# A long convolution with experts: 54 columns combined in the main loop, a ninth place for x, and another order of blocks

## The chip, the cores and the metric

The kernel runs on one core of a Trainium2 chip. Times are microseconds of device time, lower is better. The engines are named as in the profile: PE is TensorE's matmul (PEld its weight loads), DVE is VectorE, ACT is ScalarE, POOL is GpSimd, and SP is the queue from which nearly all transfers are issued.

## The reference

Inputs are `x` and `v` of 4 batches, 12608 positions and 128 channels, all float32. A small network over positions makes one long filter for each channel; `x * v` is convolved with it and gated with `x`, and then 128 positions of each batch, those with the highest scores, go through a two-layer expert.

```python
h = (np.maximum(pos_emb @ w1, 0) @ w2) * np.exp(-0.01 * pos)[:, None]
u = x * v
L = 2 * S
y = np.fft.irfft(np.fft.rfft(u, n=L, axis=1) * np.fft.rfft(h, n=L, axis=0)[None], n=L, axis=1)[:, :S]
a = x * y
scores = np.einsum('bsd,d->bs', a, w_gate)
for b in range(4):
    top = np.argpartition(-scores[b], 128)[:128]
    g = 1 / (1 + np.exp(-scores[b, top]))
    a[b, top] += g[:, None] * (np.maximum(a[b, top] @ mw1, 0) @ mw2)
```

## The kernel before

**Stages.** The Fourier transforms are written as matrix products over a grid of 101 x 250 points. After the filter's own transform (to about 120 us) comes the *main loop*: 128 steps, 32 for each of the 4 batches, each step with 4 channels. A step on PE is `f_s1` (L426), `dft` (L268) and, three steps later for the same channels, `f_i` (L263). DVE multiplies by the filter (L432 to L447). GpSimd has five instructions a step: `f_sd` (L453, L454), the product `x * v` for a later step (`stage_u`, L249), and `f_c` (L496, L497).

`f_i` leaves its result in PSUM; ACT copies it to `big`, which is read as `ay` (L477), and the last columns' second half to a small buffer `stg` (L478). For each of 126 columns `ay` holds two parts, called C and S here. `f_c` replaces them, for the columns from `JM` on, by their difference and sum. `JM` is 80 before, so these are 46 columns, 184 elements for 4 channels.

**The column loop** (class `P1`, once for each batch, after the batch's 32nd `f_i`) makes the second transform, column by column. The columns lie in 16 blocks of 8 (the last has 6), a block in two half-blocks of 4; `h` counts half-blocks in the order in which they are done, and the table `ORD` is the order of the blocks. A column whose sum and difference are there needs two products (L542); any other needs four (L546). In the profile every float32 product is two records, so 4 or 8 passes a column. For the blocks below `JB` the four middle columns are combined inside the loop, by `comb` on GpSimd (L529, two instructions of 512 elements a block), into one of two rooms of `cm`, in turn. `CB` lists these blocks in order.

For each half-block `fin` multiplies with x on DVE (L557). When a block is complete it is written out (L580, a transfer of 420 KB on SP). Then the scores are made: `weigh` multiplies with the gate's weights (L591), on DVE, or on GpSimd for the half-blocks that are `far`: those of the blocks from 10 on, but for the ones in `DW`. ACT sums each column (`sums`, L601, two records a column). For `h` of 28 and more the sums are put off into the next main loop, except in the last batch.

**Rooms for x.** The blocks of x are loaded (L519) into rooms listed in `XB`, by place in the order: one room in `wx`, five in `xa`, and two (`XE`) that lie in buffers of the main loop. Blocks whose first room isn't one of `XE` are loaded ahead, in halves, one half in each of the steps of the main loop that `LA` names; the two in `XE` when the loop begins; the others when an earlier block's write has left the room.

**What sets the order.** Everything is written in program order, and each engine's queue and SP's run in that order; the waits between them follow from the memory that the instructions touch. Besides GpSimd's waits for the loop's data, a load or a combination into a room waits for the write that still reads it. PE has four places in PSUM for half-blocks in the column loop (three in the last batch). While the main loop of one batch runs, the top-128 search of the batch before it is strung into its steps on PE, DVE and ACT, and gathers its rows by a transfer on GpSimd's queue (L899).

The second pass of rooms `XB[i]`, and the first writes of buffers that are read before they are full, need cleared memory; ACT clears these rooms in the first three steps (L1059, L1063).

Of the kernel before, what the change touches and what calls it, by code (L numbers as in the profile page):

```python
# [17 lines left out]
B, S, D, FO = 4, 12608, 128, 64  # L18
# [11 lines left out]
HB = 4  # L30
# [7 lines left out]
NU, NV, NX, NH = 4, 2, 5, 3  # L38
# [2 lines left out]
PJ = (N3 + 1) // 2  # L41
NC, CO = 4, 2
NE = 3
LA = range(32 - 14, 32 - 2)
NS, ND = 64, 4
NWARM = 8
JB = 10
JM = 8 * JB
ORD = (0, 10, 1, 2, 11, 3, 4, 12, 5, 6, 13, 7, 8, 14, 9, 15)
CB = [k for k in ORD[1:] if k < JB]  # L50
PC = 4
NL, NM = 28, 7
DW = (2, 14)
OFF, _o = {}, 0
for _n, _k, _w in (("te", 2, 2 * HC), ("qs", 2, HC), ("mt", 1, 2 * HC), ("yz", 2, 2 * HC), ("ws", 1, 728), ("sd", 2, 2 * HC),
                   ("ht", NH, 2 * HC), ("xa", NX, 8 * D), ("wx", 2, HB * D), ("cm", 2, 2 * NC * D), ("x", NU, XC), ("v", NV, XC)):
# [4 lines left out]
XE = [CE, OFF["yz"][0] + 2 * HC]  # L61
CE = [XE[0] + 8 * D, XE[1] + 8 * D]
XB = [OFF["xa"][0] + k * 8 * D for k in range(NX)] + XE
XB = [OFF["wx"][0]] + [XB[(i + NX - 2) % (NX + 2)] for i in range(len(ORD) - 1)]
AHEAD = [i for i in range(NX + 3) if XB[i] not in XE]
POS0, HID0 = 0, PJ * N1


# [95 lines left out]
def hyena_moe(ctx, tc, xg, x2, pos, bw, ww, wg, mw1, mw2, fo, c1, gx, cf, ci, wm, tk, out):  # L164
# [66 lines left out]
    blk = [c for c, _, _ in _steps()[1]]  # L231
# [267 lines left out]
    blocks = [(j0, min(j0 + 8, NJ)) for j0 in range(0, NJ, 8)]  # L499
    hbs = [(ja, min(HB, z - ja)) for a, z in (blocks[k] for k in ORD) for ja in range(a, z, HB)]  # L500

    class P1:
# [46 lines left out]
        def fin(self, h):  # L549
            ja, n = self.hbs[h]  # L550
            blk = ja // 8
            xa = self.xa[blk]
            js = slice(ja % 8, ja % 8 + n)
            end = self.last and n == 2
            if end:
                self.weigh()
            nc.vector.tensor_tensor(out=xa[:, js], in0=self.s4.pop(h)[:, :n], in1=xa[:, js], op=ALU.mult)  # L557
            if not end:
                self.weigh()
                far = ja >= JM and n == HB and h not in DW  # L560
                if h >= NL and not self.last:
                    o = OFF["cm"][0] + 2 * NC * D if h < 30 else OFF["wx"][0]
                    wx = view(arena, o + h % 2 * HB * D, [128, HB, D])
                elif far:
                    wx = view(arena, CE[self.pw % 2], [128, HB, D])
                    self.pw += 1
                else:
                    wx = view(arena, self.wx[2 + self.nw % 2 if self.nw < 6 else (self.nw - 6) % 4], [128, HB, D])
                    self.nw += 1
                self.mul = xa[:, js], wx[:, :n], ja, n, far, h  # L570
                if far:
                    self.weigh()
            else:
                for k in range(n):
                    nc.vector.scalar_tensor_tensor(out=junk, in0=xa[:, ja % 8 + k], scalar=1.0,
                                                   in1=self.wg, op0=ALU.mult, op1=ALU.mult,
                                                   accum_out=self.sc[:, ja + k:ja + k + 1])
            if ja + n == blocks[blk][1]:
                j0, j1 = blocks[blk]
                nc.sync.dma_start(out[self.b, :, j0:j1], xa[P0:P0 + PR, :j1 - j0])  # L580
                i = ORD.index(blk)
                if i > 1:
                    self.load_a(i - 1 + NX + len(XE))
                if blk in CB:
                    self.comb()

        def weigh(self):
# [19 lines left out]
        def run(self, ex):  # L607
            self.last = ex is not None
            self.ring = (0, 1, 2) if ex else (3, 2, 0, 1)
            self.wx = [OFF["wx"][0], OFF["wx"][0] + HB * D, OFF["te"][0] + (2 * HC if ex else 0),  # L610
                       OFF["sd"][0] if ex else OFF["ht"][0] + ((self.b + 1) * NG + 2) % NH * 2 * HC]
            self.wg = ps2(1, [128, D], f"wg_{self.b}")
            nc.scalar.copy(out=self.wg, in_=wgb)
            for i in range(NX + 3):
                if i not in AHEAD:
                    self.load_a(i)
            for k in range(2):
                self.comb()
            for h in range(len(self.hbs)):
                self.mm(h)  # L620
                self.fin(h)
                if h == 29:
                    stage_u((self.b + 1) * NG + 5)
                if ex:
                    ex.hook(h, self.wg)
            self.weigh()
            if ex:
                self.mask()
# [411 lines left out]
    for t in range(NT + LAG):  # L1040
        g = t % NG
        i = t - LAG
        if 0 <= i:
            f_i(i, sd.pop(i))
        if t < NT:
            pq = ps2(1 - t % 2, [128, 2, 512], f"pq_{t}")
            spare[0] = [a[:, 512 - NS:] for a in bank1]
            uv[t] = pq[:, :, :HC]
            bg.now = t
            qs = dft(t, te.pop(t), (uv[t][:, 0], uv[t][:, 1]))  # L1050
            bg.hook("p", 1)
            bg.hook("n", 1)
            if t + 1 < NT:
                te[t + 1] = f_s1(t + 1)
            spare[0] = None
            bg.hook("w", 1)
            load_u(t + NU)
            for k in range(2 * t, min(2 * t + 2, NX)):
                nc.scalar.activation(out=buf("xa", k, [128, 8 * D]), in_=one.to_broadcast([128, 8 * D]), func=AF.Copy,  # L1059
                                     scale=0.0)  # L1060
            if t == 2:
                for o, w in ((XB[0], 8 * D), (OFF["ws"][0], 728)):
                    nc.scalar.activation(out=view(arena, o, [128, w]), in_=one.to_broadcast([128, w]), func=AF.Copy,  # L1063
                                         scale=0.0)
            o = t - 1 in uv
            if o:
                y = f_y(t - 1, uv[t - 1], f_m(t - 1, uv.pop(t - 1)))
            f_v(uv[t], qs)
            for _ in range(ND):
                bg.hook("d")  # L1070
            f_u(uv[t], qs)
            seam = i >= 0 and i % NG == NG - 1
            if seam:
                f_c(i)
            if o or t - 1 in ys:
                sd[t - 1] = f_sd(t - 1, y if o else ys.pop(t - 1))
            if i < 0 or i % NG < NG - 1:
                stage_u(t + 3)
            if i >= 0 and not seam:
                f_c(i)  # L1080
            if t:
                load_h(t + 2)
            for _ in range(NE):
                bg.hook("e")
            if i >= 0 and i % NG == NG - 1:
                ys[t] = f_y(t, uv[t], f_m(t, uv.pop(t)))
            if t == NT - 1:
                sd[t] = f_last(t, uv.pop(t))
# [13 lines left out]
        b = i // NG  # L1102
        if i >= 0 and i % NG in LA:
            if i % NG == LA[0]:
                ph[b] = P1(b)
            k, e = divmod(LA.index(i % NG), 2)
            ph[b].load_a(AHEAD[k], e * HB, (e + 1) * HB)
# [59 lines left out]
```

## Time and profile before

| | |
|---|---|
| time, median of 3 runs | 899.78 us (898.28 to 901.48) |
| the profiled execution | 897.32 us, span 895.5 us |
| PE, PEld | 865.7 us (97%), 763.4 us (85%) |
| DVE, POOL, ACT | 807.6 us (90%), 763.9 us (85%), 627.9 us (70%) |
| chain that ended last | PE 71%, DVE 16%, ACT 5%, POOL 4% |
| DMA | 195.06 MB, mean 218 GB/s |

The times are of whole executions; the span is what the profile covers, the rest lies before and after it. Busy shares are averages over stages that differ: the transform of the filter, the main loop with its four column loops, and the end of the last batch.

### The profile page before, as it was taken

The page shows a single profiled execution, that of the slowest core. Times are in us where ns is not written, and L with a number is a line of the kernel's source. Part 1 is how long each engine was busy: PE and PEld are TensorE (multiplying, and loading weights), DVE is VectorE, ACT ScalarE, POOL GpSimd, SP SyncE. Part 2 cuts the span into 40 slices and gives each one's busy share as a digit, 9 for nine tenths or more (in the row PEclk, how much of TensorE's full clock was granted, in tenths as well). Part 3 has the DMA queues.
Part 4 walks back from the last instruction along what each step waited for, and adds up shares of the span by engine and source line. Part 5 has one row for each costly group of instructions (what it writes and reads, how often), then busy time and mean ns, then how long its engine had stood idle before and what let it go on. Part 6 is the DMA issues. An engine that isn't in the chain of part 4 may idle for free.

```text
span 895.5 us, 46412 instructions
## 1 busy us (share of the span) xinstructions
PE 865.7 (97%) x19606; PEld 763.4 (85%) x19606; DVE 807.6 (90%) x1543; ACT 627.9 (70%) x2242; POOL 763.9 (85%) x834
## 2 busy tenths in 40 slices
PE   8999989999999999999999999999999999999965
PEld 6788768999999889888899798888998898879954
DVE  8998899999999899999998898999998989997883
ACT  6655575555558988885579798855698888646920
POOL 5898659999999889898999798999998989988710
PEclk9999999999999999999999999999999999999996
DMA  7044587777887967688779766788797767855810
GB/s 251 35 174 172 205 291 226 213 217 230 262 248 246 296 219 220 200 247 250 243 234 299 224 213 207 231 247 236 250 300 237 221 199 227 253 176 179 267 60 7
DMA packets 83512, 195.06 MB, mean 218 GB/s; under 512 B 9639, under 2 KB 46608, under 8 KB 83304
## 3 DMA queue, kind: packets, MB, share of 16 engines
q1 hardware_dynamic: 83048, 191.57, 67.6%
q8 instruction: 154, 2.52, 1.1%
q0 software_dynamic: 256, 0.52, 0.2%
q14 instruction: 54, 0.44, 0.2%
HBM read 151.46 MB, written 40.60 MB: 214 GB/s over the span
## 4 chain that ended last, share of the span: by engine, by line
PE 71%; DVE 16%; ACT 5%; POOL 4%; issue 3%; DMA 2%; POOLq 0%; DVEq 0%; SPq 0%; ACTq 0%
PE c L263 19%; PE a L426 15%; PE c L268 15%; ACT arena L601 4%; PE c L546 3%; PE a L542 3%; PE a L546 3%; PE c L542 3%; PE c L402 2%; PE a L382 2%; DVE arena L440 2%; DVE c L441 2%; PE c L382 2%; DVE arena L446 1%; DVE ms L696 1%
## 5 line engine op out<-in xcount | busy, mean ns | idle before, releaser
L263 PE MATMUL c<-ci_sb,arena 128*26 128x126 f32 x8128 | 261.0, 271 | 2.1 <-POOL arena L453 1.6
L263 PEld LDWEIGHTS c<-ci_sb,arena 128*26 128x26 f32 x8128 | 244.7, 104 | 5.1 <-POOL arena L453 1.8
L268 PE MATMUL c<-arena,cf_sb 128*32 128x404 f32 x2048 | 214.0, 502 | 3.3 <-ACT arena L428 1.3
L426 PE MATMUL a<-c_sb,arena 128*32 128x202 f32 (+1 forms) x4096 | 216.1, 334 | 0.0
L426 PEld LDWEIGHTS a<-c_sb,arena 128*32 128x32 f32 (+1 forms) x4096 | 174.5, 108 | 26.7 <-issue 12.8
L249 POOL TENSOR_TENSOR arena<-arena 128x500 f32<-128x500 f32 x128 | 161.9, 1265 | 11.3 <-DMA arena<-in_xg_dram 11.3
L428 ACT COPY arena<-a 128x404 f32<-128x404 f32 x256 | 128.1, 501 | 50.2 <-PE a L426 48.8
L477 ACT COPY big<-c 128x824 f32<-128x824 f32 x127 | 106.3, 837 | 78.2 <-PE c L263 77.9
L453 POOL TENSOR_TENSOR arena<-arena 128x404 f32<-128x404 f32 x127 | 124.0, 977 | 39.0 <-DVE arena L447 30.7
L601 ACT ACTIVATE arena<-arena 128x128 f32<-128x128 f32 x502 | 147.4, 299 | 11.7 <-DVE arena L591 9.5
L268 PEld LDWEIGHTS c<-arena,cf_sb 128*32 128x32 f32 x2048 | 100.8, 109 | 35.6 <-issue 18.8
L440 DVE TENSOR_TENSOR arena<-c,arena 128x808 f32<-128x808 f32 x127 | 126.8, 998 | 3.8
L441 DVE TENSOR_TENSOR c<-c,arena 128x808 f32<-128x808 f32 x127 | 126.7, 998 | 0.0
L454 POOL TENSOR_TENSOR arena<-arena 128x404 f32<-128x404 f32 x127 | 123.6, 973 | 0.0
L601 ACT ACTIVATION_READ_ACCUMULATOR arena<-arena 128x1 f32 x502 | 96.0, 191 | 0.0
L529 POOL TENSOR_TENSOR arena<-big 128x512 f32<-128x512 f32 x72 | 89.8, 1285 | 0.7 <-PE c L542 0.4
L446 DVE TENSOR_TENSOR arena<-c,arena 128x404 f32<-128x404 f32 x127 | 73.6, 579 | 12.9
L435 DVE TENSOR_TENSOR c<-c,arena 128x404 f32<-128x404 f32 x128 | 74.6, 583 | 11.6 <-ACT arena L271 8.2
L432 DVE TENSOR_TENSOR c<-c,arena 128x404 f32<-128x404 f32 x128 | 75.0, 586 | 9.6 <-ACT c L765 4.9
L497 POOL TENSOR_TENSOR big<-big,arena 128x184 f32<-128x184 f32 x128 | 74.5, 582 | 10.0
L271 ACT COPY arena<-c 128x404 f32<-128x404 f32 x128 | 63.6, 497 | 24.2 <-PE c L268 23.1
L496 POOL TENSOR_TENSOR big<-big,arena 128x184 f32<-128x184 f32 x128 | 75.0, 586 | 1.3 <-ACT arena L478 1.3
(196 smaller groups left out, 1433.5 us busy)
## 6 DMA issues: line engine op xcount, KB each, us to landing
arena<-in_xg_dram SPq DMA_DIRECT2D x256, 250.0 KB, 3.9
arena<-hd SPq DMA_DIRECT2D x128, 404.0 KB, 4.5
out_dram<-arena SPq DMA_DIRECT2D x60, 420.0 KB, 5.4
arena<-in_x_dram SPq DMA_DIRECT2D x36, 420.0 KB, 4.7
hd<-arena SPq DMA_DIRECT2D x32, 404.0 KB, 3.0
arena<-in_x_dram SPq DMA_DIRECT2D x48, 210.0 KB, 5.0
arena<-in_pos_dram SPq DMA_DIRECT2D x15, 202.0 KB, 4.5
arena<-in_x_dram SPq DMA_DIRECT2D x4, 315.0 KB, 4.5
```

The source lines that it names most:

```text
L249: nc.gpsimd.tensor_tensor(out=x, in0=x, in1=v, op=ALU.mult)
L263: nc.tensor.matmul(o[32 * k:32 * k + c.stop - c.start], lhsT=lhsT[:, c], rhs=rhs, start=True, stop=True)
L268: nc.tensor.matmul(pq[w][a:a + 32], lhsT=cf_sb[:, 2 * w + a // NQ, a % NQ:a % NQ + 32], rhs=te[:, a // NQ], start=True, stop=True)
L426: nc.tensor.matmul(tps[s // 2][c, s % 2], lhsT=u[:, s, c], rhs=c1_sb[:, 0:k + 2:k + 1], start=True, stop=True)
L428: nc.scalar.copy(out=te[:, :, 2 * h:2 * h + 2].rearrange("p e s i -> p s e i"), in_=tps[h])
L440: nc.vector.tensor_tensor(out=mt, in0=uv, in1=ht[:, 0].unsqueeze(1).to_broadcast([128, 2, HC]), op=ALU.mult)
L441: nc.vector.tensor_tensor(out=uv, in0=uv, in1=ht[:, 1].unsqueeze(1).to_broadcast([128, 2, HC]), op=ALU.mult)
L453: eng.tensor_tensor(out=nat(sd[:, 0]), in0=nat(yz[:, 0]), in1=rev(yz[:, 1]), op=ALU.add)
L454: eng.tensor_tensor(out=nat(sd[:, 1]), in0=rev(yz[:, 0]), in1=nat(yz[:, 1]), op=ALU.subtract)
L477: nc.scalar.copy(out=ay[:, t % NG, :NJ + JM, ss], in_=o3[:, :, :NJ + JM].rearrange("p s x -> p x s"))
L529: nc.gpsimd.tensor_tensor(out=cm[:, e].rearrange("p j (g s) -> p j g s", s=4), in0=av[0], in1=av[1], op=op)
L601: nc.scalar.activation(out=x, in_=x, func=AF.Copy, accum_out=self.sc[:, j:j + 1])
```

## The change

`JB` is 9, so `JM` is 72: 54 columns (216 elements) are combined by `f_c` in the main loop. Block 9 needs two products for all its columns, and `comb` has 8 blocks instead of 9 in each column loop. A new constant `JF` keeps `far` at blocks from 10 on; `DW` names three half-blocks instead of two, so GpSimd weighs 8 of them in a loop and DVE 24.

The second room of `cm`, unused in the main loop, becomes the ninth place for x: it holds the block that is second in the order, block 10. Seven blocks instead of six are loaded ahead, so `LA` has 14 steps. As that room is taken when the column loop begins, only one combination stands ahead of the loop; the second, for block 2, follows block 1 and goes into the room that block 10 leaves, and each later one follows a block in turn. The order of the blocks becomes `0, 10, 1, 11, 12, 2, 3, 13, 4, 5, 14, 6, 7, 9, 8, 15`. The put-off sums of half-blocks 28 and 29 use another room. ACT clears one more room of 1024 elements in step 2.

```diff
-LA = range(32 - 14, 32 - 2)
+LA = range(32 - 16, 32 - 2)
...
-JB = 10
+JB, JF = 9, 80
 JM = 8 * JB
-ORD = (0, 10, 1, 2, 11, 3, 4, 12, 5, 6, 13, 7, 8, 14, 9, 15)
+ORD = (0, 10, 1, 11, 12, 2, 3, 13, 4, 5, 14, 6, 7, 9, 8, 15)
...
-DW = (2, 14)
+DW = (2, 6, 8)
...
-XB = [OFF["wx"][0]] + [XB[(i + NX - 2) % (NX + 2)] for i in range(len(ORD) - 1)]
-AHEAD = [i for i in range(NX + 3) if XB[i] not in XE]
+XB = [OFF["wx"][0], OFF["cm"][0] + 2 * NC * D] + [XB[(i + NX - 2) % (NX + 2)] for i in range(len(ORD) - 2)]
+AHEAD = [i for i in range(NX + 4) if XB[i] not in XE]
...
-                far = ja >= JM and n == HB and h not in DW
+                far = ja >= JF and n == HB and h not in DW
                 if h >= NL and not self.last:
-                    o = OFF["cm"][0] + 2 * NC * D if h < 30 else OFF["wx"][0]
+                    o = XB[9] if h < 30 else OFF["wx"][0]
...
-                if i > 1:
+                if i > 2:
                     self.load_a(i - 1 + NX + len(XE))
-                if blk in CB:
+                if blk in CB or i == 3:
                     self.comb()
...
-            for i in range(NX + 3):
+            for i in range(NX + 4):
                 if i not in AHEAD:
                     self.load_a(i)
-            for k in range(2):
-                self.comb()
+            self.comb()
...
             if t == 2:
-                for o, w in ((XB[0], 8 * D), (OFF["ws"][0], 728)):
+                for o, w in ((XB[0], 8 * D), (XB[1], 8 * D), (OFF["ws"][0], 728)):
```

What stands in GpSimd's list at the start of the first column loop, before. L529 are the combinations (two instructions for a block), L591 the weighings of far half-blocks; the names in brackets are semaphores, those with DMA count transfers.

```order
L453 TENSOR_TENSOR arena<-arena 128x404 [waits DVE_49,PE_49]
L454 TENSOR_TENSOR arena<-arena 128x404 [waits PE_49]
L529 TENSOR_TENSOR arena<-big 128x512 [waits Pool_49]
L529 TENSOR_TENSOR arena<-big 128x512 x3
L591 TENSOR_TENSOR arena<-arena,wgb 128x512 [waits DMAHW2_49,DVE_49]
L529 TENSOR_TENSOR arena<-big 128x512 [waits PE_49,Pool_49] x4
L591 TENSOR_TENSOR arena<-arena,wgb 128x512 [waits DMAHW2_49,DVE_49]
L591 TENSOR_TENSOR arena<-arena,wgb 128x512 [waits DVE_49,Activation_49,Pool_49]
```

Two blocks are combined at once, then half-block 3 is weighed, and two more combinations wait for PE alone.

The same place in GpSimd's list after the change:

```order
L453 TENSOR_TENSOR arena<-arena 128x404 [waits DVE_49,PE_49]
L454 TENSOR_TENSOR arena<-arena 128x404 [waits PE_49]
L529 TENSOR_TENSOR arena<-big 128x512 [waits Pool_49]
L529 TENSOR_TENSOR arena<-big 128x512
L591 TENSOR_TENSOR arena<-arena,wgb 128x512 [waits DMAHW4_49,DVE_49]
L529 TENSOR_TENSOR arena<-big 128x512 [waits DMAHW6_49,DMAHW0_49,DVE_49]
L529 TENSOR_TENSOR arena<-big 128x512 [waits Pool_49]
L591 TENSOR_TENSOR arena<-arena,wgb 128x512 [waits DMAHW4_49,DVE_49]
L529 TENSOR_TENSOR arena<-big 128x512 [waits PE_49] x2
L591 TENSOR_TENSOR arena<-arena,wgb 128x512 [waits DMAHW3_49,DVE_49,Activation_49]
L529 TENSOR_TENSOR arena<-big 128x512 [waits PE_49,Pool_49] x4
```

One block is combined ahead; the second combination, behind the weighing of half-block 3, waits for transfers, and the weighings of half-blocks 7 and 9 stand behind it with the third combination between them.

SP's list there after the change, from the two loads that the loop begins with. Each transfer waits for its own semaphore's last use, and the semaphores go round from 0 to 7, so the second write below, block 10's, is the one that DMAHW6 counts:

```order
L519 DMA arena<-in_x_dram 105x1024 [waits DMAHW3_49,DVE_49,Activation_49]
L519 DMA arena<-in_x_dram 105x1024 [waits DMAHW4_49,Pool_49]
L580 DMA out_dram<-arena 105x1024 [waits DMAHW5_49,DVE_49]
L580 DMA out_dram<-arena 105x1024 [waits DMAHW6_49,DVE_49]
L580 DMA out_dram<-arena 105x1024 [waits DMAHW7_49,DVE_49]
L580 DMA out_dram<-arena 105x1024 [waits DMAHW0_49,DVE_49]
L519 DMA arena<-in_x_dram 105x1024 [waits DMAHW7_49,DMAHW1_49]
```

Before, the first load inside the loop followed the third write and waited for block 10's; now it follows the fourth and waits for block 1's (DMAHW7).

ACT's list in step 2 of the main loop, after the change:

```order
L1058 ACTIVATE arena<-one 128x1024
L1062 ACTIVATE arena<-one 128x1024
L1062 ACTIVATE arena<-one 128x1024 [waits DMAHW4_49,DMAHW3_49]
L1062 ACTIVATE arena<-one 128x728 [waits DMAHW7_49,DMAHW1_49,DMAHW0_49]
L477 COPY big<-c_74 128x792 [waits PE_49]
L478 COPY arena<-c_74 128x216
```

Before it had one clear of 1024 less at L1063 (the lines stand one higher now), and the two copies had 824 and 184 elements.

## The prediction

> **What bounds the kernel now.** I read the page first, then busy time by stage, the groups by form, and the timelines of PE, GpSimd, ACT and SP at the places that the change touches.
>
> ```profile
> span 895.5 us, 46412 instructions
> PE 865.7 (97%) x19606; PEld 763.4 (85%) x19606; DVE 807.6 (90%) x1543; ACT 627.9 (70%) x2242; POOL 763.9 (85%) x834
> PE 71%; DVE 16%; ACT 5%; POOL 4%; issue 3%; DMA 2%; POOLq 0%; DVEq 0%; SPq 0%; ACTq 0%
> ```
>
> PE (TensorE) is 97% busy and holds 71% of the chain that ended last: whatever idles PE is paid in full, and whatever another engine gains is paid only where PE waits for it. The stretches below are the four column loops (b=0 to 3) and five main steps.
>
> ```profile
> 266.60:303.80 37.20, 37.20 (x681) 37.05 (x680) 34.85 (x56) 32.59 (x219) 35.29 (x30) 1.00 0.82 257
> 448.30:486.60 38.30, 37.66 (x683) 37.27 (x680) 35.66 (x58) 31.67 (x211) 37.60 (x34) 1.00 0.83 260
> 632.80:670.60 37.80, 37.63 (x681) 37.26 (x680) 35.20 (x57) 31.66 (x211) 37.07 (x33) 1.00 0.85 270
> 810.40:852.60 42.20, 41.40 (x729) 40.65 (x730) 34.39 (x64) 37.31 (x252) 34.81 (x29) 1.00 0.76 235
> 379.50:400.90 21.40, 21.40 (x566) 18.79 (x560) 20.46 (x40) 18.21 (x58) 21.01 (x26) 1.00 0.81 239
> ```
>
> Columns: window, its length, then busy time of PE, PEld, DVE, ACT, POOL, granted clock, DMA. The first three loops last as long as PE's 680 matmul passes: 37.2 us / 680 = 54.7 ns each. In the fourth ACT decides: its sums (L601) run through on the chain.
>
> ```profile
> 815.51 16.69 ACT arena L601 x112
> 832.56 18.39 ACT arena L601 x125
> ```
>
> 112 records are 56 sums, so 298 ns a sum.
>
> **The change, part by part.** The costs come from these groups.
>
> ```profile
> L249 POOL TENSOR_TENSOR arena<-arena 128x500 f32<-128x500 f32 x128 | 161.9, 1265 | 11.3 <-DMA arena<-in_xg_dram 11.3
> L497 POOL TENSOR_TENSOR big<-big,arena 128x184 f32<-128x184 f32 x128 | 74.5, 582 | 10.0
> L529 POOL TENSOR_TENSOR arena<-big 128x512 f32<-128x512 f32 x72 | 89.8, 1285 | 0.7 <-PE c L542 0.4
> L591 POOL TENSOR_TENSOR arena<-arena,wgb 128x512 f32<-128x512 f32 x36 | 46.0, 1296 | 9.7 <-ACT arena L601 4.6 <-DMA out_dram<-arena 3.6 <-DVE arena L557 0.7
> L591 DVE TENSOR_TENSOR arena<-arena,c 128x512 f32<-128x512 f32 x88 | 59.7, 678 | 1.7 <-ACT arena L601 1.7
> L1059 ACT ACTIVATE arena<-one 128x1024 f32<-128x1024 f32 x5 | 5.1, 1054 | 0.0
> L477 ACT COPY big<-c 128x824 f32<-128x824 f32 x127 | 106.3, 837 | 78.2 <-PE c L263 77.9
> L478 ACT COPY arena<-c 128x184 f32<-128x184 f32 x127 | 39.7, 313 | 0.0
> ```
>
> *Matmuls saved.* Block 9 falls from 48 passes to 32 in every column loop: 16 x 54.7 ns = 0.87 us, in full in the first three loops; in the fourth ACT hides it.
>
> *`f_c` in the main loop.* 184 to 216 elements, twice a step. From 184 to 500 elements GpSimd takes (1265 - 582) / 316 = 2.16 ns an element, so +69 ns an instruction, +0.14 us a step. What room is there? From the timelines of GpSimd and PE (start, length):
>
> ```profile
> 379.56 0.57 POOL L496 TENSOR_TENSOR big<-big,arena 128x184 f32<-128x184 f32 x1
> 383.84 0.57 POOL L496 TENSOR_TENSOR big<-big,arena 128x184 f32<-128x184 f32 x1
> ...
> 375.86 1.94 PE L263 MATMUL c<-ci_sb,arena 128*26 128x126 f32 x64
> 380.34 1.95 PE L263 MATMUL c<-ci_sb,arena 128*26 128x126 f32 x64
> ```
>
> Where GpSimd runs without a gap its step is 4.28 us, PE's 4.48. With 4.42 it stays under PE and catches up more slowly: nothing on the path. If all 582 ns grew with the elements (3.16 ns each), +101 ns an instruction make 4.48, level with PE; then at most 0.02 us a step, 2.5 us over some 125 steps. Ends: 0 and +2.5; I take 0, since two contiguous sizes of the same operation give the slope.
>
> *The copies.* 824 to 792 and 184 to 216: ACT's total of 1008 elements stays, 837 - 26 and 313 + 26 ns by the slope between them. Zero.
>
> *Clearing the new room* (once, step 2). The rows of ACT, then of PE:
>
> ```profile
> 125.08 1.74 ACT L1063 ACTIVATE arena<-one 128x1024 f32<-128x1024 f32 x2
> 126.72 0.83 ACT L477 COPY big<-c 128x824 f32<-128x824 f32 x1
> 127.44 0.32 ACT L478 COPY arena<-c 128x184 f32<-128x184 f32 x1
> ...
> 127.91 1.35 PE L263 MATMUL c<-ci_sb,arena 128*26 128x126 f32 x41
> ```
>
> Five clears of this size (L1059 above) keep ACT 5.1 us, 1.0 each. The next L263 writes the PSUM tile that L477 and L478 empty; L478 ends at 127.76, 0.15 before PE starts there. One more clear moves it to 128.8: PE starts 0.9 us later, once. **+0.9** (ends 0, if the clear fell into a gap of ACT's, and 1.05; the rows show no gap from 125.08 to 127.65).
>
> *The weighing moved to VectorE, the x loads.* Half-block 8 (block 12) takes 0.68 us on DVE instead of 1.29 on POOL. DVE has 2.3 us idle in the shortest loop and PE's other four PSUM places cover it. The two more half loads go out in steps that carry three DMAs each, far ahead of use; one full load less is left inside the loop. Zero for both; uncovered they would cost 0.7 and about 5 us a loop, and DVE or DMA would have to run out for that.
>
> *The second combination, behind a write.* This is the term that decides. `comb` for block 2 writes into the room where block 10's x stood, which block 10's output write reads until it lands. GpSimd stops at that wait, and behind it in order stand the weighing of half-block 7, the combination of block 3 and the weighing of half-block 9; PE waits for the combinations, ACT's sums for the weighings. When the write is issued and has landed can be read off SP's timeline: in the kernel before, the next load (L519) into block 10's room waits for the same write.
>
> ```profile
> 273.76 2.12 SPq L580 DMA_DIRECT2D out_dram<-arena  x2
> 278.35 0.34 SPq L519 DMA_DIRECT2D arena<-in_x_dram  x1
> ...
> 456.28 2.25 SPq L580 DMA_DIRECT2D out_dram<-arena  x2
> 461.12 0.34 SPq L519 DMA_DIRECT2D arena<-in_x_dram  x1
> ...
> 640.52 2.12 SPq L580 DMA_DIRECT2D out_dram<-arena  x2
> 644.81 0.34 SPq L519 DMA_DIRECT2D arena<-in_x_dram  x1
> ...
> 817.30 2.33 SPq L580 DMA_DIRECT2D out_dram<-arena  x2
> 820.28 0.95 SPq L519 DMA_DIRECT2D arena<-in_x_dram  x1
> ```
>
> 4.59, 4.84, 4.29 and 2.98 us from issue. Blocks 0, 10 and 1 stand at the head of both orders, so these times hold. On GpSimd four combinations in a row take 4.98 us, 1.24 from start to start. Below are rows of its timeline, PE's timeline (start, length; in brackets idle time and what ended it), and one of the list of waits (us in total, times, longest):
>
> ```profile
> 268.67 4.98 POOL L529 TENSOR_TENSOR arena<-big 128x512 f32<-128x512 f32 x4
> ...
> 452.93 4.95 POOL L529 TENSOR_TENSOR arena<-big 128x512 f32<-128x512 f32 x4
> ...
> 266.55 3.71 PE L546 MATMUL c<-big,gx_sb 128*64 128x128 f32 x64
> ...
> 455.47 0.54 PE L542 MATMUL c<-arena,gx_sb 128*64 128x128 f32 x5 [0.64 <-POOL arena L529]
> ...
> PE c L542 <- POOL arena L529: 0.8, 2, 0.6
> ```
>
> Loop 0: block 2 is combined at 278.40 + 2.50 = 280.9. PE needs it after 64 (block 0) + 32 + 48 + 32 + 32 + 16 = 224 passes, at 266.6 + 12.25 = 278.85: it waits 2.05 us. Then PE has 48 passes (2.62 us) to the first combined column of block 3, GpSimd a weighing and two combinations (3.72): 1.10 more. From there to block 8 PE has 336 passes (18.38 us), GpSimd five weighings and ten combinations (18.6): 0.2. PE ends 1.3 us plus 440 passes (24.07) after 280.9: 306.3, so 39.7 us instead of 37.2: **+2.5**. The saved 0.87 is in this.
>
> Loop 1: 461.17 + 2.50 + 25.37 = 489.0, 40.7 instead of 38.3: **+2.4**. Loop 2: 644.86 + 27.87 = 672.7, 39.9 instead of 37.8: **+2.1**. PE's old wait of 0.64 us for the first combination (loop 1, above; 0.8 in all by the waits) is swallowed, however late it gets: one combination less stands ahead, but some five `f_c` pairs of +0.14 us lie ahead of it too.
>
> Loop 3: the write lands after 3 us, block 2 is combined at 822.8, half-block 7 weighed at 824.05, half-block 9 at 827.8. ACT, from 815.51, is through its first 28 sums at 823.85 and waits 0.25; two half-blocks of sums later (826.5) it waits 1.3; at half-blocks 14 and 20 another 0.5. Its sums end the loop: **+2.1** (with a write of 4.6 us, +3.7).
>
> Sum: 2.5 + 2.4 + 2.1 + 2.1 + 0.9 = +10.0 us on the profiled execution's 897.32 us (span 895.5 and 1.8 around it), so 907.3. The median shown, 899.78, lies 2.5 above that execution; on it the forecast is **909.8 us**, 1.1% slower.
>
> **Rivals.**
>
> *The write lands in 3 us everywhere.* The fourth loop shows 2.98 us, with the main loop's loads gone. Then block 2 is combined at 279.3, 461.8 and 646.1, the loops grow by 0.8, 0.6 and 0.8, and with 2.1 and 0.9 the sum is +5.2: 905.0. Against it: three loops in three take 4.3 to 4.8 us, and the change leaves the traffic there as it is. The Trainium skill (DMA: Bandwidth & Descriptors, section Anatomy of one DMA — SWDGE (gpsimd) path) gives a DMA a fixed 2.0 us, mostly the receipt of its last byte, plus its bytes at 436 GB/s; for a block of 430,080 bytes that makes, as an estimate, 3.0 us, and the time would be this rival's 905.0 instead of 909.8. The fourth loop's 2.98 agrees with the rule, the other three loops do not.
>
> *The wait is hidden (not slower).* If the write had landed when GpSimd comes to it, PE would keep its 16 passes: 3 x 0.87 less, the old waits of 0.8 us for a combination perhaps gone, 0.9 for the clear and some 0.6 for GpSimd's later turns: about -1.9, 897.9. This decides if the write is down by 276.3, 2.5 us after issue in loop 0. All four rows are above that, and GpSimd's list shows the wait at this place; it could fall only if VectorE came to block 10 earlier.
>
> *GpSimd bounds the main loop.* It decides once an `f_c` instruction grows by more than 0.10 us. At +0.15 a step is 4.58 against 4.48: 0.1 x 125 = 12 us more, 922. For it: GpSimd is 21.01 of 21.40 us busy above. Against it: the slope, and gaps in many other steps.
>
> **How the numbers follow.** The forecast 0.68, the 3 us write 0.11, the hidden wait 0.12, GpSimd in the main loop 0.09. About 0.3%, 2.7 us, is what a measurement here can tell from no change. Slower: the forecast, the first and third rival, 0.88; of the hidden wait's 0.12 I put 0.07 within 0.3% and 0.05 on faster. Range: from the 3 us write (905.0, less 0.5) to writes of the 5.4 us that is the median of all output writes (+0.8 in each of three loops) with `f_c` at its dear end (+2.5): 914.7. **904.5 to 915.**
>
> ```profile
> out_dram<-arena SPq DMA_DIRECT2D x60, 420.0 KB, 5.4
> ```
>
> **What would show it.** Right: POOL idle some 3.4 us ahead of the third L529 in each of the first three loops, ended by DMA out_dram; PE's L542 waiting for POOL L529 twice a loop, 2 to 3 and 1.1 us, 10 us or more in all where it was 0.8; ACT L601 waiting for POOL L591 some 3 us a loop; loops of 39.7, 40.7 and 39.9; main steps still some 4.48 us with L497 at 0.65. Wrong: no wait at L542, loops of 36.3 us (the hidden wait); L263 waiting for L453 through the main loop (GpSimd the bound); no later L263 in the first steps (the clear free).

## The result, and the profile after

The changed kernel takes 911.0 us (median of four runs, 909.78 to 914.37); its ratio to the kernel before is 1.0137, with a 95% interval of 1.0112 to 1.0162. Run again beside the variants below it took 909.83 us, ratio 1.0122 (1.0102 to 1.0142). The forecast was 909.8. Of all executions here one, of nine places alone, took 2240.7 us; it is left out of that kernel's ratio.

From the page of the changed kernel, the lines that answer to those shown of before:

```profile
span 912.3 us, 46288 instructions
PE 869.8 (95%) x19542; PEld 761.0 (83%) x19542; DVE 809.5 (89%) x1547; ACT 629.4 (69%) x2243; POOL 765.0 (84%) x822
PE 62%; DVE 19%; POOL 6%; ACT 5%; DMA 4%; issue 4%; POOLq 0%; DVEq 0%; ACTq 0%
```

PE's share of the chain that ended last fell from 71% to 62%, and GpSimd's rose to 6%. The column loops, three from PE's first pass to its last, the fourth to ACT's last sum (columns as in the prediction's windows):

```profile
273.97:313.57 39.60, 37.51 (x669) 36.47 (x672) 35.33 (x57) 31.74 (x209) 32.09 (x27) 1.00 0.81 259
459.27:498.91 39.64, 37.92 (x671) 36.66 (x672) 35.21 (x57) 31.82 (x209) 33.65 (x30) 1.00 0.83 265
644.16:684.73 40.57, 38.12 (x670) 36.63 (x672) 36.09 (x59) 31.83 (x209) 34.61 (x31) 1.00 0.81 263
823.69:867.72 44.03, 41.63 (x715) 40.34 (x715) 34.80 (x65) 37.49 (x252) 31.01 (x26) 1.00 0.75 233
```

PE is busy 37.5 to 38.1 us of 39.6 to 40.6, where it stood still for at most 0.6 us of a loop before. What it waits for stands in the timelines of SP, GpSimd and PE at the first loop: block 10's output write, the combinations (L529) and the passes that read them (L542), with the idle time and what ended it in brackets.

```profile
281.17 0.34 SPq L580 DMA_DIRECT2D out_dram<-arena  x1
...
276.48 2.49 POOL L529 TENSOR_TENSOR arena<-big 128x512 f32<-128x512 f32 x2
281.23 1.28 POOL L591 TENSOR_TENSOR arena<-arena,wgb 128x512 f32<-128x512 f32 x1 [2.25 <-DVE arena L557]
285.61 2.49 POOL L529 TENSOR_TENSOR arena<-big 128x512 f32<-128x512 f32 x2 [3.10 <-DMA out_dram<-arena]
...
286.94 0.43 PE L542 MATMUL a<-arena,gx_sb 128*64 128x128 f32 x2 [0.52 <-POOL arena L529]
288.16 0.54 PE L542 MATMUL a<-arena,gx_sb 128*64 128x128 f32 x5 [0.79 <-POOL arena L529]
...
291.83 0.54 PE L542 MATMUL c<-arena,gx_sb 128*64 128x128 f32 x5 [0.78 <-POOL arena L529]
```

The write is issued at 281.17 and GpSimd goes on at 285.61, 4.4 us later, after 3.10 us of idleness. PE then stops at block 2, once for the sum and once for the difference, and again at block 3. In loops 1 and 2 the same place reads

```profile
470.90 1.27 POOL L529 TENSOR_TENSOR arena<-big 128x512 f32<-128x512 f32 x1 [3.26 <-DVE arena L591]
656.74 2.48 POOL L529 TENSOR_TENSOR arena<-big 128x512 f32<-128x512 f32 x2 [3.26 <-DVE arena L591]
```

Here the profile names VectorE, but it is the write again. The weighing that it names in loop 1 (469.76 to 470.44) stands behind this combination in program order, and VectorE's last use of the room ended at 466.88, before GpSimd stood still. The writes were issued at 466.32 and 652.14, 4.6 us before GpSimd went on. From the list of waits, in us in all, times and longest:

```profile
ACT arena L601 <- POOL arena L591: 11.5, 15, 1.7
PE a L542 <- POOL arena L529: 3.7, 5, 0.8
PE c L542 <- POOL arena L529: 3.1, 4, 0.8
PEld a L542 <- POOL arena L529: 5.2, 7, 1.0
PEld c L542 <- POOL arena L529: 5.2, 8, 1.0
```

Profiles of one execution differ by some us for other reasons (last section), so the account is made between the second profile of each kernel, spans 897.5 and 906.8 us, in which the main loop starts within 0.5 us of the same time. "Other main steps" is the time from the first `dft` to the last column loop, less the three loops and, where the clear stands in step 2, less the 0.94 us that it adds.

| us | before | changed | more | forecast |
|---|---|---|---|---|
| up to the first main step | 114.98 | 114.49 | -0.5 | 0 |
| clear of the new room (step 4 of PE) | 4.49 | 5.46 | +1.0 | +0.9 |
| column loop 0 | 37.33 | 39.67 | +2.3 | +2.5 |
| column loop 1 | 38.43 | 39.81 | +1.4 | +2.4 |
| column loop 2 | 38.24 | 40.51 | +2.3 | +2.1 |
| column loop 3, to the last sum | 42.28 | 44.06 | +1.8 | +2.1 |
| other main steps | 583.4 | 584.4 | +1.0 | 0 |
| after the last sum | 42.9 | 42.9 | 0 | 0 |

### The profile page after: what moved, and what is told of

The parts are those of the page before. It is cut to its first block, busy times and chain, and to the rows that moved or that the text cites. A ratio compares the mean times of both kernels' runs of the same rounds, so it can differ in the third digit from the quotient of the medians.

```text
span 912.3 us, 46288 instructions
## 1 busy us (share of the span) xinstructions
PE 869.8 (95%) x19542; PEld 761.0 (83%) x19542; DVE 809.5 (89%) x1547; ACT 629.4 (69%) x2243; POOL 765.0 (84%) x822
## 4 chain that ended last, share of the span: by engine, by line
PE 62%; DVE 19%; POOL 6%; ACT 5%; DMA 4%; issue 4%; POOLq 0%; DVEq 0%; ACTq 0%
PE c L263 19%; PE a L426 15%; PE c L268 15%; DMA hd<-arena 4%; ACT arena L601 3%; PE a L542 3%; DVE arena L410 3%; PE c L546 2%; PE c L542 2%; PE a L546 2%; DVE arena L440 2%; DVE c L441 2%; POOL arena L529 1%; DVE ms L695 1%; DVE c L408 1%
## 5 line engine op out<-in xcount | busy, mean ns | idle before, releaser
L263 PE MATMUL c<-ci_sb,arena 128*26 128x126 f32 x8128 | 263.8, 270 | 2.8 <-issue 0.9
L268 PE MATMUL c<-arena,cf_sb 128*32 128x404 f32 x2048 | 217.2, 502 | 3.3 <-DVE arena L447 0.9
L426 PE MATMUL a<-c_sb,arena 128*32 128x202 f32 (+1 forms) x4096 | 219.5, 334 | 0.0
L426 PEld LDWEIGHTS a<-c_sb,arena 128*32 128x32 f32 (+1 forms) x4096 | 176.5, 108 | 27.1 <-issue 10.0
L477 ACT COPY big<-c 128x792 f32<-128x792 f32 x127 | 102.7, 809 | 76.7 <-PE c L263 76.3
L497 POOL TENSOR_TENSOR big<-big,arena 128x216 f32<-128x216 f32 x128 | 83.1, 649 | 10.0
L529 POOL TENSOR_TENSOR arena<-big 128x512 f32<-128x512 f32 x64 | 79.6, 1274 | 11.4 <-DVE arena L591 8.2
L496 POOL TENSOR_TENSOR big<-big,arena 128x216 f32<-128x216 f32 x128 | 83.5, 652 | 0.2 <-ACT arena L478 0.2
```

The source lines that it names most:

```text
L263: nc.tensor.matmul(o[32 * k:32 * k + c.stop - c.start], lhsT=lhsT[:, c], rhs=rhs, start=True, stop=True)
L268: nc.tensor.matmul(pq[w][a:a + 32], lhsT=cf_sb[:, 2 * w + a // NQ, a % NQ:a % NQ + 32], rhs=te[:, a // NQ], start=True, stop=True)
L426: nc.tensor.matmul(tps[s // 2][c, s % 2], lhsT=u[:, s, c], rhs=c1_sb[:, 0:k + 2:k + 1], start=True, stop=True)
L477: nc.scalar.copy(out=ay[:, t % NG, :NJ + JM, ss], in_=o3[:, :, :NJ + JM].rearrange("p s x -> p x s"))
L529: nc.gpsimd.tensor_tensor(out=cm[:, e].rearrange("p j (g s) -> p j g s", s=4), in0=av[0], in1=av[1], op=op)
```

## The experiments

The theory: the landing of the write that still reads the second room of `cm` sets when block 2 is combined, and from there the column loop runs on a fixed schedule. Its main rival: the new order and the single combination ahead give GpSimd too much to do, whatever the write does.

### The changed kernel and the kernel before, once more

> The changed kernel once more, unedited, as the base of its variants. 911.0 us again, 1.2 to 1.5% over the kernel before. In its profile the stretch ahead of the first main step, which the change leaves alone and which was 5.4 us later in the first profile (f_i(0) at 128.8 instead of 123.4), should be back within 1 us of the kernel before if that was a matter of one execution; if it is 5 us late again, the change has moved something there that the forecast does not hold.

Measured: 909.83 us, 1.0122 (1.0102 to 1.0142), and the first main step at 114.5 us where the first profile of this kernel had 118.7. So the 5.7 us by which that profile started late were of one execution.

> The kernel before once more, for a second profile of it. If the first profile, 2.5 us under the median, was one with few single late steps: column loops of 37.3, 38.4 and 37.9 again within 0.4, and PE's waits that the profile puts to nothing (issue) at 1.5 to 4 us in the main loop where the first had 0.8; main loop's first step at 113 to 117 us.

Measured: 899.28 us in its one run; loops of 37.33, 38.43 and 38.24; first main step at 114.98; PE's waits put to issue 1.8 us. As expected, the profile that the forecast was made from had few late steps.

### Which write the combination waits for: rooms exchanged

Block 0's x in the second room of `cm`, block 10's in `wx`; nothing else.

```diff
-XB = [OFF["wx"][0], OFF["cm"][0] + 2 * NC * D] + ...
+XB = [OFF["cm"][0] + 2 * NC * D, OFF["wx"][0]] + ...
```

> The changed kernel with two rooms exchanged: block 0's x stands in the second room of the combinations, block 10's in the room of the weighings. The second combination then waits for the output write of block 0, which is issued some 2.4 us before that of block 10; orders and amounts of work are unchanged. Theory (the landing of the write sets when block 2 is combined): PE's wait of about 2 us at block 2 goes, about 0.8 at block 3 and 0.2 at block 8 stay; first three loops 2.3 us shorter each, the fourth 1.2 (ACT waits less for far weighings): about 8 us less than the changed kernel, 903. Rival (GpSimd's own amount of work in the new order sets PE's waits, not the write): the loops stay at 39 to 40 us, 911. The weighing of half-block 8 now waits on VectorE for block 10's write; if that is not covered, the gain is 1 to 2 us a loop smaller.

Block 0's write and the second combination in the timelines of SP and GpSimd, then the windows of the first three loops:

```profile
275.02 0.34 SPq L580 DMA_DIRECT2D out_dram<-arena  x1
...
279.81 2.50 POOL L529 TENSOR_TENSOR arena<-big 128x512 f32<-128x512 f32 x2 [1.05 <-DMA out_dram<-arena]
```

```profile
270.20:307.81 37.61, 37.04 (x670) 36.45 (x672) 35.16 (x57) 31.64 (x209) 32.25 (x28) 1.00 0.80 253
453.88:492.68 38.80, 37.34 (x670) 36.52 (x672) 35.36 (x57) 31.76 (x209) 33.26 (x29) 1.00 0.85 272
642.22:680.68 38.46, 37.31 (x670) 36.49 (x672) 35.27 (x57) 31.78 (x209) 31.72 (x27) 1.00 0.81 257
```

Measured: 907.37 us, ratio 1.0082 (1.0061 to 1.0103). GpSimd's wait for the write is 1.1, 2.2 and 1.9 us in the three loops. The loops are 2.1, 1.0 and 2.1 us shorter than in the repeated changed kernel, the last sum 1.0 earlier, 6.2 in all. For the loops the rival falls: order and work are those of the changed kernel. But the time fell by only 2.5 us by the medians (3.6 by the ratios), and the expected 903 was missed; in the profiles the main steps outside the loops took 589.1 us instead of 584.4, so most of the rest was given back there.

### The other way: the room given to block 1

```diff
-XB = [OFF["wx"][0], OFF["cm"][0] + 2 * NC * D] + [XB[...] ... - 2)]
+XB = [OFF["wx"][0]] + [XB[...] ... - 2)]
+XB[2:2] = [OFF["cm"][0] + 2 * NC * D]
```

> The changed kernel with the new room given to block 1 instead of block 10: the second combination then waits for the output write of block 1, which in the changed kernel's profile is issued 1.8 us after that of block 10 and lands after 3.95 us (282.97 to 286.92). Order and work unchanged. Theory (the landing sets when block 2 is combined): the third L529 starts 1.3 us (that landing) to 1.8 us (landing in 4.4) later, the first three loops are 1.3 to 1.8 longer, 41.2, 41.4 and 42.1, and ACT ends the fourth 1.3 to 1.8 later: 911 + 6 = 917. With the exchange of rooms (block 0's write, issued 2.4 earlier, loops 2.0, 0.9 and 2.1 shorter) that would make three points on one line. Rival (the order's load on GpSimd sets the waits): 911.

Measured: 925.04 us, 1.0266 (1.0241 to 1.0290), loops of 42.6, 43.8 and 44.8. This edit did two things at once. The combination is written ahead of the weighing of block 1's second half, so that weighing read the combination instead of a product with x, and VectorE waited 21.6 us in all for GpSimd there: a second new wait beside the one under test, so the time says nothing of the theory. The variant that does this weighing first:

```diff
+                if i == 2:
+                    self.weigh()
                 if blk in CB or i == 3:
                     self.comb()
```

> The new room given to block 1, mended: the weighing of block 1's second half is done ahead of the combination that overwrites its room, so that VectorE no longer waits for GpSimd there. The second combination waits for block 1's output write, issued 1.8 us after block 10's (278.21 and 276.41 in the repeated changed kernel). Theory (the landing of the write sets when block 2 is combined): third L529 1.3 to 1.8 us later, loops of 41.0 to 41.5, 41.1 to 41.6 and 41.8 to 42.3 us where the changed kernel has 39.7, 39.8 and 40.5, ACT's last sum 1.8 later in the fourth: 910.5 + 6 = 916.5. Rival (the order's load on GpSimd sets the waits): 910.5.

Block 1's write and the second combination (the lines stand one lower here), then the windows:

```profile
277.89 0.33 SPq L581 DMA_DIRECT2D out_dram<-arena  x1
...
281.81 2.47 POOL L530 TENSOR_TENSOR arena<-big 128x512 f32<-128x512 f32 x2 [4.38 <-DMA out_dram<-arena]
```

```profile
268.88:309.79 40.91, 37.55 (x670) 36.48 (x672) 35.30 (x57) 31.74 (x209) 32.20 (x28) 1.00 0.79 254
456.76:497.17 40.41, 37.55 (x671) 36.47 (x672) 34.67 (x56) 31.74 (x209) 32.38 (x28) 1.00 0.80 254
642.12:684.78 42.66, 38.17 (x670) 36.63 (x672) 36.08 (x59) 31.82 (x209) 34.64 (x31) 1.00 0.79 244
```

Measured: 917.67 us, 1.0184 (1.0161 to 1.0208), about the expected 916.5. The loops are 1.2, 0.6 and 2.1 us longer than in the repeated changed kernel: the first just under the expected stretch, the second 0.7 under it (block 1's write landed 3.4 us after issue there), the third 0.4 over it. ACT's last sum in the fourth loop came 2.6 us later, not 1.8.

### The write in halves

```diff
+            if blk == ORD[1] and ja % 8 == 0:
+                nc.sync.dma_start(out[self.b, :, ja:ja + n], xa[P0:P0 + PR, :n])
...
-                nc.sync.dma_start(out[self.b, :, j0:j1], xa[P0:P0 + PR, :j1 - j0])
+                a = HB if blk == ORD[1] else 0
+                nc.sync.dma_start(out[self.b, :, j0 + a:j1], xa[P0:P0 + PR, a:j1 - j0])
```

> The changed kernel with block 10's output write issued in two halves of 210 KB, the first when its first half-block is done. The second is issued when the whole write was. Theory one (the landing takes time for the bytes of the write itself): the second half lands 0.5 to 1.2 us earlier after its issue than the 4.4 to 4.6 us of the whole, each of the first three loops that much shorter, 907 to 909. Theory two (the landing is set by what stands ahead in the queue and by a fixed part): no change in the loops, 910.5.

The two writes and the second combination in loop 0:

```profile
275.01 0.34 SPq L579 DMA_DIRECT2D out_dram<-arena  x1
...
276.21 0.86 SPq L583 DMA_DIRECT2D out_dram<-arena  x1
...
280.30 2.49 POOL L529 TENSOR_TENSOR arena<-big 128x512 f32<-128x512 f32 x2 [2.75 <-DMA out_dram<-arena]
```

Measured: 909.88 us, 1.0098 (1.0060 to 1.0137): in time inconclusive (the same as the repeated changed kernel by the medians, 2 us less by the ratios). In the trace, the first halves land 5.1, 5.1 and 4.8 us after issue, the second 4.5, 4.5 and 4.3: half the bytes take as long as the whole write's 4.4 to 4.6. That speaks against theory one; no run separates the two parts of theory two. The third L529 starts 0.4 to 1.3 us earlier against the loop's start in loops 0 and 2, since its first instruction overwrites only the first half (issued 1.2 us sooner; in loop 0 it landed at 280.13, the second at 280.67); in loop 1 a late first combination undid that.

**Five kernels on one line.** When the third L529 starts and how long the loop lasts, both from PE's first pass of the loop:

| third L529 starts / loop lasts, us | loop 0 | loop 1 | loop 2 |
|---|---|---|---|
| rooms exchanged | 9.6 / 37.6 | 10.8 / 38.8 | 10.5 / 38.5 |
| write in halves | 11.3 / 39.3 | 12.1 / 40.1 | 11.2 / 39.2 |
| changed kernel | 11.6 / 39.6 | 11.6 / 39.6 | 12.6 / 40.6 |
| the same, repeated | 11.7 / 39.7 | 11.9 / 39.8 | 12.5 / 40.5 |
| room of block 1, weighed first | 12.9 / 40.9 | 12.4 / 40.4 | 14.7 / 42.7 |

The second number less the first is 28.0 in all fifteen, within 0.06. So what stands behind that combination runs on a fixed schedule, and the landing that it waits for sets the loop's length one for one.

### Nine places alone, in the old structure

```diff
-JB = 10
+JB, JF = 9, 80
...
-                far = ja >= JM and n == HB and h not in DW
+                far = ja >= JF and n == HB and h not in DW
```

> The kernel before with one part of the change alone: nine blocks combined by GpSimd instead of ten that are not formed in the main loop (JB 9, near blocks as before), old rooms, old order, two combinations ahead of each column loop. Theory (f_c's extra 0.14 us a step is free, the 16 passes saved per column loop are paid out in the first three): loops of 36.3, 37.4 and 36.9 us, 2.6 us less, 896.4. Rival one (GpSimd bounds the main loop): main step 4.58 instead of 4.48, +10 us, about 906. Rival two (f_c costs a little in many steps, where GpSimd is already behind): +2.5, so about 899, no change. In the theory PE's wait for the subtraction sums of L453 stays as it was.

Measured: 899.05 us, ratio 0.9998 (0.9985 to 1.0010). The loops (36.47, 37.10 and 37.84) gained 2.3 us on the first profile of before, about what was expected; the time gained nothing. Hence once more:

> Nine places alone in the old structure once more. Its first profile had column loops of 36.5, 37.1 and 37.8 us where the kernel before had 37.3, 38.4 and 37.9, 2.3 us less, and equal main steps but for single ones 0.3 to 0.9 us longer, yet the time was that of the kernel before. Theory (the saving is real and small beside chance delays of single steps): loops as in that profile, the long steps at other places, time 0 to 2.6 us under the kernel before. Rival (f_c's added time makes the same steps late in each execution): long steps again at 63, 64, 70, 71, 103 and 121.

Windows of the first three loops, then rows of PE's list of waits, from the second run:

```profile
267.85:304.32 36.47, 36.47 (x670) 36.30 (x672) 34.81 (x56) 31.76 (x213) 32.38 (x29) 1.00 0.81 259
452.13:488.59 36.46, 36.46 (x671) 36.29 (x672) 34.27 (x55) 31.41 (x209) 32.78 (x29) 1.00 0.82 251
636.07:673.88 37.81, 37.02 (x669) 36.45 (x672) 35.43 (x57) 30.94 (x206) 34.55 (x32) 1.00 0.84 265
```

```profile
PE c L263 <- issue: 4.2, 5, 1.4
PE c L268 <- issue: 1.1, 1, 1.1
```

Measured: 900.57 us, 1.0001 (0.9982 to 1.0020). In sum the loops of the two runs lie 2.6 and 3.3 us under those of the second profile of before (111.4 and 110.7 against 114.0), and the main steps outside took 586.0 and 589.3 us instead of 583.7 and 583.4. Step by step most main steps (106 and 100 of 124) agree within 0.025 us with those before; the excess lies in a dozen or so single steps. Some of them are at the same places in both profiles (62 to 64, 70 and 71, 102 and 103, 121 and 122), some are not, so neither expectation holds cleanly.

### Eight places alone

The same edit with `JB, JF = 8, 80`.

> The kernel before with eight places (C and S of 62 columns formed in the main loop), near blocks, rooms and order as before. f_c at 248 elements is 582 + 64 x 2.06 = 714 ns by the slope measured between 184 and 216, GpSimd's step without a gap 4.28 + 4 x 0.066 = 4.54 us against PE's 4.46 to 4.48. Theory (GpSimd becomes the bound once its step is longer than PE's): steps of 4.54 in the main loop, PE waiting for L453, 0.07 x 120 = 8 us lost, 3 x 1.7 = 5 us saved in the column loops: 903. Rival one (f_c is free as long as no step is stretched, and GpSimd's 0.06 a step is caught up somewhere): 895. Rival two (already nine places lost 2 us in the main loop, and eight lose twice that): 899.

Timelines of PE and GpSimd in the first main loop, then of PE in the first column loop:

```profile
225.63 2.01 PE L263 MATMUL c<-ci_sb,arena 128*26 128x126 f32 x64
230.18 2.03 PE L263 MATMUL c<-ci_sb,arena 128*26 128x126 f32 x64
234.75 2.01 PE L263 MATMUL c<-ci_sb,arena 128*26 128x126 f32 x64
...
227.05 0.73 POOL L496 TENSOR_TENSOR big<-big,arena 128x248 f32<-128x248 f32 x1
231.60 0.73 POOL L496 TENSOR_TENSOR big<-big,arena 128x248 f32<-128x248 f32 x1
...
275.67 1.97 PE L542 MATMUL a<-big,gx_sb 128*64 128x128 f32 x32 [0.61 <-POOL big L497]
279.95 0.54 PE L542 MATMUL c<-arena,gx_sb 128*64 128x128 f32 x5 [0.78 <-POOL arena L529]
```

Measured: 906.13 us, 1.0064 (1.0043 to 1.0084). GpSimd's step is 4.55 us, as worked out (4.54), and from the 19th step on PE's is the same instead of 4.45. But that holds only to the end of the first batch's steps, 15 of them: 1.6 us, not 8. In the later batches single longer steps of PE (4.7 to 5.5) keep GpSimd level until the last one or two. Most of the price is at the head of the column loops, where GpSimd arrives late: PE waits for `f_c` and for the first combination, and the loops last 38.1 us where 648 passes of 54.7 ns make 35.4. The theory had the amount (903) nearly right and the place wrong.

### Ten places in the new structure

```diff
-JB, JF = 9, 80
+JB, JF = 10, 80
```

> The changed kernel without its part in the main loop: ten blocks combined by GpSimd again (JB 10), rooms, order and waits as changed. Block 9 has 48 passes again and a combination, which goes in front of block 8's. Theory: +0.87 us of passes and, since GpSimd is already behind when it comes to blocks 9 and 8, some 1.7 us of PE waiting for the combination of block 9: +2.6 in each of the first three loops, the fourth unchanged (ACT), f_c back at 585 ns: 911 + 7.8 = 919. Rival one (only the passes count): 913.5. Rival two (f_c's extra 66 ns an instruction had cost 2 us in the main loop): 2 less than either.

Measured: 916.98 us, 1.0171 (1.0144 to 1.0199). Loops of 42.3, 42.3 and 43.9 us, 2.6, 2.5 and 3.4 over the changed kernel, as the theory says (PE waits at block 9 as well); in time 7 us by the medians of the two kernels, 4.4 by their ratios. By the medians that lies between the theory (7.8) and rival two (5.8), by the ratios below both, so it does not settle what `f_c` costs.

### The clear in later steps

```diff
-                for o, w in ((XB[0], 8 * D), (XB[1], 8 * D), (OFF["ws"][0], 728)):
+                for o, w in ((XB[0], 8 * D), (OFF["ws"][0], 728)):
...
+            if 8 <= t < 12:
+                nc.scalar.activation(out=view(arena, XB[1] + (t - 8) * 2 * D, [128, 2 * D]), ...)
```

> The changed kernel with the clearing of the new room taken out of step 2 and done in four pieces of 256 elements in steps 8 to 11. Theory: ACT has room there, the step from f_i(0) to f_i(1) falls from 5.46 to 4.52 us, the others stay, 0.9 us less: 909.6. Rival (the pieces delay the copies in steps 8 to 11): those steps longer by 0.2 each, no gain.

PE's f_i(0) and f_i(1) in the changed kernel, then in this one:

```profile
128.82 1.95 PE L263 MATMUL c<-ci_sb,arena 128*26 128x126 f32 x64
134.28 1.93 PE L263 MATMUL c<-ci_sb,arena 128*26 128x126 f32 x64 [0.77 <-ACT arena L478]
```

```profile
125.19 1.95 PE L263 MATMUL c<-ci_sb,arena 128*26 128x126 f32 x64
129.72 1.93 PE L263 MATMUL c<-ci_sb,arena 128*26 128x126 f32 x64
```

Measured: 909.32 us, 1.0090 (1.0067 to 1.0112). f_i(1) has lost its wait for L478, the step is 4.53 us instead of 5.46, and steps 8 to 11 are 4.45 us as before: the clear cost 0.9 us because of where it stood. The time, 0.5 us less by the medians and 2.9 by the ratios, can't show so little.

### Exchanged rooms, block 9 early, the clear later

```diff
-ORD = (0, 10, 1, 11, 12, 2, 3, 13, 4, 5, 14, 6, 7, 9, 8, 15)
+ORD = (0, 10, 1, 11, 9, 2, 12, 3, 4, 13, 5, 6, 14, 7, 8, 15)
```

> The rooms exchanged as above, the blocks in the order 0, 10, 1, 11, 9, 2, 12, 3, 4, 13, 5, 6, 14, 7, 8, 15 (block 9, which needs no combination and no GpSimd weighing, goes ahead of block 2), and the clearing of the new room in four pieces in steps 8 to 11. Theory: no wait of PE for a combination after the first, loops of 36.3, 37.2 and 36.5, the fourth as in the kernel before, no 0.9 us for the clear: about 2.6 us less than the kernel before, 896.4. Rival one (f_c is not free in the main loop): as much above 896.4 as nine places alone are. Rival two (the write of block 0 still lands too late at the new place): +1 us a loop, 899 to 900.

Measured: 899.96 us, ratio 0.9994 (0.9975 to 1.0014); loops of 36.6, 37.5 and 37.7, the last sum at 42.0. All of the changed kernel's loss is undone, and the loops are 2.1 us shorter in sum than in the second profile of before; but nothing of that is seen in the time. In loops 1 and 2 PE still waits 0.5 and 0.7 us at block 2, which is rival two at half its price. The profile is that of the slowest of its 12 executions (906.78 us), so the loops may be compared but not the rest. No variant beats the kernel before.

## Why the prediction was right

**The wait, its place and its price.** Third L529 behind block 10's write, 3.1 to 3.3 us idle (forecast 3.4); the write landing after 4.4 to 4.6 us in three loops (4.6, 4.8 and 4.3 taken) and 2.9 in the fourth (2.98 taken); loop length equal to the start of that combination plus 28.0 (the forecast's working gives 27.87). That the cause is the write, and not the order, is shown by moving the wait to an earlier and to a later write.

**The size of each loop.** Loop 0 is right to 0.1. Loop 1 was forecast at 40.7 and lasts 39.6 to 39.8: the time of the write's issue was carried over from the profile of before (8.0 us after PE's start), where PE had stood 0.64 us for the first combination ahead of it; after the change it is 7.1 to 7.2. The prediction called that wait swallowed in words but left it in the term ("these times hold"). The landing took 4.6 us, not 4.8. Loop 2 was forecast at 39.9 and lasts 40.5 to 40.6: there GpSimd comes out of the main loop late (first combination 5.0 to 5.1 us after PE's start, 4.2 to 4.5 before), PE waits for it, and the write is issued at 8.0 us, not at the 7.7 taken. It lands after 4.6, not 4.3, so about half of this error is the landing. The lag with which GpSimd enters a loop, left out, and a landing read from one execution thus make one loop too long and one too short; that they nearly cancel is luck.

**The total.** The forecast had +7.0 us for the first three loops, which are 6.0 longer, and nothing for the other main steps, which are 1.0 longer in this pair of profiles. That the sum is right to 1.2 us, and to 0.03 in the repeat, is in part luck too.

**A sign that came out smaller.** PE's waits for L529 were to make 10 us or more in all. Its list has 6.8 (3.7 and 3.1), that of its weight loads 10.4.

**Loop 3.** ACT's last sum comes 1.8 us later (forecast 2.1); its waits for far weighings were 0.25, 1.23 and 0.18, where the last had been put at 0.5.

**The clear** cost 0.9 as forecast, and moving it took it away.

**`f_c` in the main loop.** The row of the changed kernel:

```profile
L497 POOL TENSOR_TENSOR big<-big,arena 128x216 f32<-128x216 f32 x128 | 83.1, 649 | 10.0
```

+67 ns an instruction where 69 were worked out, and GpSimd's step without a gap is 4.39 us (385.24 to 389.63 between two L496) under PE's 4.45 to 4.48. Undisturbed main steps did not get longer. So the term of 0 stands for these steps; the "other main steps" are 1.0 us longer in the changed kernel, and 2.5 to 6 longer with nine places alone, which the prediction's dear end (+2.5) covers only in part. Whether `f_c` has a share in that is not shown. The expected 3 x 0.87 us of saved passes are in the loops, but alone they gave no gain in time: the step "in full in the first three loops" holds for the loops and not for the kernel. Where the rest went is told only in part by the last section.

**Rivals.** The 3 us write is excluded by all three loops. Half of the write and the whole of it landed after 4.3 to 5.1 us, so under this loop's traffic the bytes of the write are not what its landing waits for. By the Trainium skill (DMA: Bandwidth & Descriptors, section Anatomy of one DMA — SWDGE (gpsimd) path), whose rule is for transfers that GpSimd issues while SP issues these, half the bytes would land after an estimated 2.5 us instead of 3.0; the first three loops do not agree. The hidden wait needed the write down by 276.3 on the old clock, and no landing came near. GpSimd as the bound of the main loop begins at eight places (4.55 us steps), as its condition says.

## What to carry to other kernels

When a buffer that is being written out is reused, what counts is the landing of the write and what stands in order behind the instruction that waits for it. Price a term that starts "when the transfer is issued" from the changed schedule, with the lag at which each engine enters, not from the time read in the old trace: that lag moved the write's issue in two of three loops, by 0.2 to 0.9 us here. And a gain that the stage shows (2 to 3 us in the loops) may not reach the kernel's time: compare the sum of the other steps too.

## What the runs showed of the hardware

PE's single late steps have a common sign. In the fourteen profiles PE has 47 waits over 0.25 us in the main loop that the profile puts to issue, and for 46 of them the trace holds a packet of the instruction queue that began 2.2 to 2.8 us before PE went on. The longest of the second run of nine places alone, and the window ahead of it from the view of transfers:

```profile
508.85 1.56 PE L263 MATMUL c<-ci_sb,arena 128*25 128x126 f32 x49 [1.41 <-issue]
```

```profile
q1 hardware_dynamic: 286, 0.64, 60.8%
q8 instruction: 1, 0.02, 1.7%
```

One packet of 16 KB was fetched in 505.5 to 509. There are 153 or 154 such packets on that queue in an execution, so chance would put about one wait in ten behind one (154 x 0.6 us of 900). PE's place in its own list says the same. Its records in the trace, weight loads included, are some 39,400, one packet for every 256, and counted in order the same 46 waits stand where the count leaves 193 or 194 when divided by 256. The one wait without such a packet stands elsewhere. If the packets are taken in order as these blocks of 256 instructions, no block of some 1,840 in the fourteen profiles begins less than 2.2 us after its packet; the median is 4.1 us where PE does not wait. So PE waits, up to 1.65 us here, where a block's packet begins too late. What makes it late is open, and no run took a fetch away. As the blocks end at fixed places of the program, late steps can recur at the same places in different executions.

These waits sum to 0.8 and 1.8 us in the two profiles of before and to 4.2 to 5.7 in the second of nine places, the exchanged rooms and the new order. The main steps outside the loops were 582.7 to 585.5 us in the kernels with long loops and in both profiles of before, 587.7 with eight places, 586.0 to 591.8 in those with nine places and short loops. But these are single executions: those of the kernel before alone lie between 895.9 and 904.4 us, and the 591.8 belongs to an execution 6.8 us over its kernel's median. So the profiles don't show that short loops make the main steps longer; that nine places alone give back the 2 to 3 us gained in the loops rests on the medians, and how is open.
